# Gate and value products over 32 attention weights, with fp32 halves stacked in the 128 rows

## The chip, the core and the metric

The kernel runs on one core of a Trainium2 chip. The metric is the device time of one execution in microseconds (us), lower is better. TensorE is called PE (its weight loads PEld), VectorE DVE, ScalarE ACT, GpSimd POOL and SyncE SP, whose queue issues the loads and stores.

## What is computed

Two blocks in a row, all in fp32. Attention: x is (4, 12416, 128), the inducing points are (32, 128).

```python
def mab(q, kv):
    s = scale * (q @ kv.transpose(0, 2, 1))
    a = np.exp(s - s.max(-1, keepdims=True))
    a /= a.sum(-1, keepdims=True) + 1e-09
    return a @ kv
h = mab(I, x)          # (4, 32, 128): the inducing points attend to x
x = mab(x, h)          # (4, 12416, 128): x attends to h
```

Then a gated FFN over all 49664 tokens, with weights 128 x 1536, 128 x 1536 and 1536 x 128:

```python
xn = x / np.sqrt(np.mean(x * x, axis=-1, keepdims=True) + 1e-06) * rms_g
g = xn @ w_gate
out = (g / (1 + np.exp(-g)) * (xn @ w_val)) @ w_out
```

A token's x in the FFN is a sum of only 32 rows of h, weighted by its attention weights.

## The kernel before

A batch has 97 blocks of 128 tokens; a unit is four blocks (512 tokens), with one block left over as unit 25. Tokens stand in the columns, the 128 features in the rows. The order of instructions on each engine is the order in which the program writes them; nothing is moved later.

The FFN of a unit (`ffn`, L378) runs 12 slots j, one for each 128 of the 1536 hidden columns. A slot makes the gate product (L403) and the value product (L405), each 128 x 512 with xnT as the moving operand, into two of the four `gv` banks of PSUM. ACT makes silu of the gate (L407), DVE multiplies it by the value (L409) into u. The output product of u (L386) is issued one slot late (`late`), after the next slot's gate and value products, and adds up in `acc` over the 12 slots. Then ACT copies `acc` (L398), and in slot 2 of the next unit PE turns it, DVE copies it (L393) and SP stores it.

Between the products of a slot, `slot` (L430) runs other work: the steps of the next batch's attention, one after another and spread evenly over 24 units, and the seam of the next unit. All of this work shares the two `mm` banks.

The seam makes xnT of a unit: `seam_turn` (slot 1) turns the attention weights of four blocks into [(block, m), token]; `seam_x` (slot 3) multiplies them with a block-diagonal h (`diag`, L348), so that x = a @ h stands with tokens in rows, and POOL squares it; `seam_rms` (slot 5) sums the squares, raises the mean to -0.5 on POOL (L362) and scales x (L364); `seam_end` (slot 8) turns the four blocks (L372) and multiplies by the rms weights (L374).

The attention of a batch: `turn_x` turns x, `scores1` (L191) makes stage 1's scores with four products that use 32 columns of the array each; `max1` to `exp1` (L234) make the exponentials, `turn_e` and `sum_h` (L261) the weighted sums, `end_h` and `turn_h` the result h. `scores2` (L304) makes stage 2's scores as [token, m], one product with 32 columns and its own weight load per block, 16 blocks to a bank; `exp2` (L316) and `norm2` (L329) finish them. The last attention lies under the third batch's FFN.

Batch 0's attention runs ahead of all FFN work and uses the `gv` banks. Between its steps `load_w` (L120) brings in the weights, which come as doubles: SP loads 512 columns, DVE makes eight operations of it and POOL the last (L149).

Of the kernel before, what the change touches and what calls it, by code (L numbers as in the profile page):

```python
# [9 lines left out]
F32 = mybir.dt.float32  # L10
I32 = mybir.dt.int32
U32 = mybir.dt.uint32
AF = mybir.ActivationFunctionType
ALU = mybir.AluOpType
# [4 lines left out]
R = 4  # sets of 32 partitions  # L19
TB = 4  # token blocks of 128 in one 512-wide tile  # L20
GB = R * TB  # token blocks in one attention group


@with_exitstack
def kernel(
# [24 lines left out]
    NG = NB // GB  # L50
    SCALE = float(1.0 / (C ** 0.5))
# [3 lines left out]
    # (first block, number of blocks, sets of blocks, blocks in each)  # L55
# [4 lines left out]
    TAIL0 = NG * TB * P  # first column of the last group's stage 1 scores  # L60
    SCW = TAIL0 + (P if tail else 0)
    units = [(j, min(TB, NB - j)) for j in range(0, NB, TB)]

# [6 lines left out]
    rawp = pool("rawp", 2)  # L70
    small = pool("small", 2)
    work = pool("work", 3)
    seam = pool("seam", 2)
    silp = pool("silp", 4)
# [24 lines left out]
    wg = const.tile([P, F], F32, name="wg")  # L99
    wv = const.tile([P, F], F32, name="wv")  # L100
    wo = const.tile([P, NJ, C], F32, name="wo")
    ident = const.tile([P, P], F32, name="ident")
# [3 lines left out]
    mhalf = const.tile([P, TB], F32, name="mhalf")  # L106
    nc.gpsimd.memset(mhalf[:], -0.5)
    # fold[(q, m), (q', m')] = [m == m']: sums over the sets, into each of them
# [10 lines left out]

    def load_w(i, c):  # L120
# [5 lines left out]
        src, dst = (moe_w_gate, moe_w_val, moe_w_out)[i], (wg, wv, wo.rearrange("p j c -> p (j c)"))[i]  # L126
        dst, k = dst[:, ts(c, 512)], 512 // C
# [4 lines left out]
        raw = rawp.tile([P, 512, 2], I32, name="raw")  # L132
        words = raw[:].rearrange("p f w -> p (f w)")
        nc.sync.dma_start(out=words if i < 2 else words.rearrange("p (j c) -> p j c", j=k), in_=src.bitcast(I32))
        low, high = raw[:, :, 0], raw[:, :, 1]
# [24 lines left out]
    sc, diag = {}, {}  # L160

    def attention(b, load_next):
        """The steps of a batch's attention, in order, up to a in sc[b] and h in diag[b]."""
# [48 lines left out]
        def max2():  # L212
            ps = bank()
            nc.tensor.transpose(ps[0:1, 0:P], st["mx"][:], ident[:])
            row = small.tile([1, m], F32, name="row")
            nc.vector.reduce_max(out=row[:], in_=ps[0:1, 0:P].rearrange("p (q m) -> p m q", m=m), axis=AX.X)
            row4 = small.tile([1, R, m], F32, name="row4")
# [12 lines left out]
        def exp1():  # L230
            s = sc[b]
            hl = st["hl"] = small.tile([P, C + 1], F32, name="hl")
            lt = small.tile([P, 1], F32, name="lt")
            nc.scalar.activation(s[:, 0:TAIL0], s[:, 0:TAIL0], AF.Exp, bias=st["nbias"][:], scale=SCALE,  # L234
                                 accum_out=hl[:, C:C + 1])
            if tail:
                nc.scalar.activation(s[0:m, TAIL0:SCW], s[0:m, TAIL0:SCW], AF.Exp, bias=st["nbias"][0:m],
# [39 lines left out]
        def end_h():  # L277
# [5 lines left out]
            h = st["h"] = small.tile([P, C], F32, name="h")  # L283
            nc.vector.tensor_scalar_mul(out=h[:], in0=ps[:, 0:C], scalar1=rec[:])
            # one block for each of a unit's four blocks of tokens
# [5 lines left out]
        def turn_h():  # L291
            ps = bank()
            nc.tensor.transpose(ps[:, 0:m], st["h"][0:m, :], ident[0:m, 0:m])
            hT = st["hT"] = small.tile([P, m], F32, name="hT")
            nc.vector.tensor_copy(out=hT[:], in_=ps[:, 0:m])

# [3 lines left out]
        def scores2(g):  # L300
            j0, nb, nq, nt = groups[g]
            ps = bank().rearrange("p (j m) -> p j m", m=m)
            for j in range(nb):
                nc.tensor.matmul(ps[:, j, :], xT[:, ts(j0 + j, P)], st["hT"][:], start=True, stop=True)  # L304
            mx = small.tile([P, GB], F32, name="mx2")
            nc.vector.reduce_max(out=mx[:, 0:nb], in_=ps[:, 0:nb, :], axis=AX.X)
            nc.vector.tensor_tensor(
                out=blocks(j0, nb), in0=ps[:, 0:nb, :],
                in1=mx[:, 0:nb].unsqueeze(2).to_broadcast((P, nb, m)), op=ALU.subtract,
            )  # L310

        def blocks(j0, nb):
            return sc[b][:, ds(j0 * m, nb * m)].rearrange("p (j m) -> p j m", m=m)
# [4 lines left out]
        for g in range(len(groups)):  # L318
            add(lambda g=g: scores2(g))
        add(exp2)  # L320

        def norm2(g):
            j0, nb, nq, nt = groups[g]
            a = blocks(j0, nb)
            l2 = small.tile([P, GB], F32, name="l2")
            nc.vector.reduce_sum(out=l2[:, 0:nb], in_=a, axis=AX.X)
            nc.vector.tensor_scalar_add(out=l2[:, 0:nb], in0=l2[:, 0:nb], scalar1=1e-9)
            nc.vector.reciprocal(out=l2[:, 0:nb], in_=l2[:, 0:nb])
            nc.gpsimd.tensor_tensor(out=a, in0=a, in1=l2[:, 0:nb].unsqueeze(2).to_broadcast((P, nb, m)), op=ALU.mult)  # L329

        for g in range(len(groups)):
            add(lambda g=g: norm2(g))
        return steps

    # The seam: xn = x / rms * g of a unit of four blocks, with x = a @ h, transposed.
    st2, xnT = {}, {}

    def seam_turn(b, u):
        j0, nt = units[u]
        ps = ps_m.tile([P, 512], F32, name="mm", tag="mm")  # L340
        nc.tensor.transpose(ps[0:nt * m, 0:P], sc[b][:, ds(j0 * m, nt * m)], ident[:])  # L341
        aT = st2["aT", b, u] = seam.tile([P, P], F32, name="aT")
        nc.vector.tensor_copy(out=aT[0:nt * m, :], in_=ps[0:nt * m, 0:P])  # L343

    def seam_x(b, u):
        j0, nt = units[u]
        ps = ps_m.tile([P, TB, C], F32, name="mm", tag="mm")
        nc.tensor.matmul(ps[:, 0:nt, :], st2.pop(("aT", b, u))[0:nt * m, :], diag[b][0:nt * m, 0:nt, :],  # L348
# [29 lines left out]
    def ffn(b, u, slot):  # L378
# [22 lines left out]
        for j in range(NJ):  # L401
# [8 lines left out]
            if j == 2 and stores:  # L410
                stores.pop()()
# [62 lines left out]
```

## Time and profile before

| what | us |
|---|---|
| median of 3 runs | 3515.55 |
| lowest and highest run | 3512.94, 3516.49 |
| span of the profiled execution | 3520.3 |
| PE busy (98% of the span) | 3443.0 |
| DVE busy (36%) | 1259.5 |
| ACT busy (24%) | 835.7 |
| POOL busy (10%) | 346.6 |

The profile records one execution. Busy times of PE are of pipelined instructions whose ends are modelled, so the distance between starts tells more than a duration. A fp32 product is recorded as two instructions.

### The profile page before, as it was taken

How to read it: one execution, taken by the hardware profiler on the slowest of the kernel's cores; microseconds unless marked ns; L12 is line 12 of the kernel's file. 1: busy time of each engine (PE TensorE's matmuls, PEld its weight loads, DVE VectorE, ACT ScalarE, POOL GpSimd, SP SyncE). 2: the span in 40 equal slices, each digit the busy share in tenths (PEclk: the TensorE clock that was granted, in tenths of full speed). 3: DMA queues.
4: the chain of work that ended last, by engine and by line, in shares of the span. 5: the costliest groups of instructions: out<-in, count | busy, mean ns of one | idle time of the engine just before them, and what ended most of it. 6: DMA issues, size and time to landing. Idle time of an engine off the chain costs nothing.

```text
span 3520.3 us, 28077 instructions
## 1 busy us (share of the span) xinstructions
PE 3443.0 (98%) x10541; PEld 1658.6 (47%) x10541; DVE 1259.5 (36%) x2209; ACT 835.7 (24%) x1398; POOL 346.6 (10%) x364
## 2 busy tenths in 40 slices
PE   5799999999999999999999999999999999999999
PEld 3644444445454444444545444444454444444444
DVE  6333333333333333333343333333334333333333
ACT  1122222221222222222122222222222222222222
POOL 1101000010110001010011101000101100110110
PEclk7699999999999999999999999999999999999999
DMA  4000000110000000010000000000000000000000
GB/s 177 23 9 7 9 6 9 42 46 7 7 10 6 9 6 9 8 55 31 7 9 7 9 7 9 10 6 10 6 7 10 7 9 6 9 9 9 6 9 10
DMA packets 21208, 57.39 MB, mean 16 GB/s; under 512 B 2352, under 2 KB 4944, under 8 KB 18000
## 3 DMA queue, kind: packets, MB, share of 16 engines
q1 hardware_dynamic: 20880, 55.58, 4.4%
q8 instruction: 82, 1.34, 0.2%
q14 instruction: 54, 0.44, 0.0%
q10 hardware_dynamic: 192, 0.02, 0.0%
HBM read 30.16 MB, written 25.43 MB: 16 GB/s over the span
## 4 chain that ended last, share of the span: by engine, by line
PE 96%; DVE 2%; ACT 1%; DMA 1%; issue 0%; POOL 0%; POOLq 0%; ACTq 0%; DVEq 0%
PE acc L386 29%; PE gv L403 28%; PE gv L405 28%; PE mm L348 2%; PE mm L304 2%; PE mm L372 1%; PE mm L391 1%; PE gv L304 1%; PE mm L183 1%; PE mm L261 1%; PE mm L191 1%; DMA raw<-in_moe_w_gate_dram 0%; PE mm L341 0%; PE mm L249 0%; PE gv L261 0%
## 5 line engine op out<-in xcount | busy, mean ns | idle before, releaser
L409 DVE TENSOR_TENSOR u<-silu,gv 128x512 f32<-128x512 f32 (+1 forms) x1200 | 805.3, 672 | 2086.1 <-PE gv L405 1869.0
L407 ACT ACTIVATE silu<-gv 128x512 f32<-128x512 f32 (+1 forms) x1200 | 700.7, 584 | 2399.8 <-PE gv L403 2381.2
L386 PE MATMUL acc<-u,wo 128*128 128x512 f32 (+1 forms) x2400 | 1207.8, 585 | 9.7 <-DVE u L409 9.7
L403 PE MATMUL gv<-xnT,wg 128*128 128x512 f32 (+1 forms) x2400 | 1202.7, 583 | 0.8 <-DVE xnT L374 0.8
L405 PE MATMUL gv<-xnT,wv 128*128 128x512 f32 (+1 forms) x2400 | 1198.4, 581 | 0.0
L403 PEld LDWEIGHTS gv<-xnT,wg 128*128 128x128 f32 x2400 | 454.8, 191 | 556.3 <-issue 554.4
L405 PEld LDWEIGHTS gv<-xnT,wv 128*128 128x128 f32 x2400 | 454.5, 191 | 555.6 <-issue 555.6
L386 PEld LDWEIGHTS acc<-u,wo 128*128 128x128 f32 x2400 | 421.5, 191 | 412.3 <-issue 383.9
L353 POOL TENSOR_TENSOR sq<-xa 128x512 f32<-128x512 f32 (+1 forms) x100 | 101.5, 1015 | 2325.6 <-DVE xa L351 2325.6
L362 POOL TENSOR_TENSOR rs<-ms,mhalf 128x4 f32<-128x4 f32 (+1 forms) x100 | 99.0, 990 | 507.2 <-DVE ms L360 502.1
L348 PE MATMUL mm<-diag,aT 128*128 128x512 f32 (+1 forms) x200 | 101.8, 590 | 6.5 <-DVE aT L343 6.5
L364 POOL TENSOR_TENSOR xa<-xa,rs 128x512 f32<-128x512 f32 (+1 forms) x100 | 101.5, 1015 | 7.9
L398 ACT COPY oT<-acc 128x512 f32<-128x512 f32 (+1 forms) x100 | 57.3, 573 | 111.0 <-PE acc L386 111.0
L374 DVE TENSOR_SCALAR xnT<-mm,gam 128x512 f32<-128x512 f32 (+1 forms) x100 | 72.9, 729 | 7.7 <-PE mm L372 7.5
L372 PEld LDWEIGHTS mm<-ident,xa 128*128 128x128 f32 x388 | 47.9, 142 | 53.8 <-issue 43.2
L351 DVE COPY xa<-mm 128x512 f32<-128x512 f32 (+1 forms) x100 | 67.3, 673 | 16.1 <-PE mm L348 7.8
L304 PEld LDWEIGHTS mm<-hT,xT 128*128 128x128 f32 x582 | 68.5, 193 | 8.6 <-issue 5.7
L391 PEld LDWEIGHTS mm<-ident,oT 128*128 128x128 f32 x388 | 48.5, 141 | 49.8 <-issue 47.7
L372 PE MATMUL mm<-ident,xa 128*128 128x128 f32 x388 | 59.7, 276 | 8.3 <-POOL xa L364 8.3
L393 DVE COPY o<-mm 128x512 f32<-128x512 f32 (+1 forms) x100 | 66.7, 667 | 1.5 <-PE mm L391 1.3
L304 PE MATMUL mm<-hT,xT 128*128 128x32 f32 x582 | 67.2, 274 | 0.0
L359 DVE TENSOR_REDUCE ms<-sq 128x4 f32<-128x512 f32 (+1 forms) x100 | 66.2, 662 | 1.6 <-POOL sq L353 1.2
(123 smaller groups left out, 812.8 us busy)
## 6 DMA issues: line engine op xcount, KB each, us to landing
xn<-in_x_dram SPq DMA_DIRECT2D x24, 1024.0 KB, 5.9
out_dram<-o SPq DMA_DIRECT2D x96, 256.0 KB, 2.0
raw<-in_moe_w_gate_dram SPq DMA_DIRECT2D x3, 512.0 KB, 12.4
raw<-in_moe_w_val_dram SPq DMA_DIRECT2D x3, 512.0 KB, 3.6
raw<-in_moe_w_out_dram SPq DMA_DIRECT2D x3, 512.0 KB, 3.9
xnt<-in_x_dram SPq DMA_DIRECT2D x4, 64.0 KB, 6.3
out_dram<-o SPq DMA_DIRECT2D x4, 64.0 KB, 1.5
ind<-in_inducing_dram ACTq DMA_DIRECT2D x1, 16.0 KB, 3.3
```

Source lines behind the costliest of these rows:

```text
L304: nc.tensor.matmul(ps[:, j, :], xT[:, ts(j0 + j, P)], st["hT"][:], start=True, stop=True)
L348: nc.tensor.matmul(ps[:, 0:nt, :], st2.pop(("aT", b, u))[0:nt * m, :], diag[b][0:nt * m, 0:nt, :], start=True, stop=True)
L353: nc.gpsimd.tensor_tensor(out=sq[:, 0:nt, :], in0=xa[:, 0:nt, :], in1=xa[:, 0:nt, :], op=ALU.mult)
L362: nc.gpsimd.tensor_tensor(out=rs[:, 0:nt], in0=ms[:, 0:nt], in1=mhalf[:, 0:nt], op=ALU.pow)
L364: nc.gpsimd.tensor_tensor(out=xa[:, 0:nt, :], in0=xa[:, 0:nt, :], in1=rs[:, 0:nt].unsqueeze(2).to_broadcast((P, nt, C)), op=ALU.mult)
L372: nc.tensor.transpose(ps[:, ts(t, P)], xa[:, t, :], ident[:])
L386: nc.tensor.matmul(acc[:, 0:T], wo[:, j, :], t[:, 0:T], start=(j == 0), stop=(j == NJ - 1))
L391: nc.tensor.transpose(ps[:, ts(t, P)], oT[:, ts(t, P)], ident[:])
L403: nc.tensor.matmul(g[:, 0:T], wg[:, ts(j, P)], xn[:, 0:T], start=True, stop=True)
L405: nc.tensor.matmul(v[:, 0:T], wv[:, ts(j, P)], xn[:, 0:T], start=True, stop=True)
L407: nc.scalar.activation(s[:, 0:T], g[:, 0:T], AF.Silu)
L409: nc.vector.tensor_tensor(out=t[:, 0:T], in0=s[:, 0:T], in1=v[:, 0:T], op=ALU.mult)
```

## The change

Gate and value products no longer take xn. Since x = a @ h, the gate is (a / rms) @ (h * rms_g) @ w_gate, and the product h * rms_g * w is made once a batch, for 32 rows. The moving operand is then the scaled attention weights, 32 rows of them. Weights and attention weights are each split in a half rounded to the type `F32R` and the rest, also as `F32R`; rows 0 to 63 of the stationary operand hold the first half twice, rows 64 to 127 the second half twice, and the moving operand holds its halves as (first, second, first, second). One product over 128 rows adds up all four half products.

- Units: the last two of a batch have 3 and 2 blocks in place of 4 and 1. Four units make a set.
- `load_w` converts a gate or value slice into a work buffer and SP stores it to DRAM (`w32`); the raw doubles lie in buffers of the scores.
- Stage 2's scores are made like stage 1's, [(q, m), token], copied, and turned (`turn_s`). `norm2` is gone.
- Six steps `stack` a batch read the slices back (`fetch`), multiply them by h and write the two halves. The attention has 75 steps in place of 68, spread over 19 units in place of 24.
- The seam works on a set: x is made only for its squares, which ACT makes; the attention weights are scaled by what also holds the softmax's sum, turned, and split on DVE. Its seven steps lie in the second and third unit of the set before.
- `gather` brings the halves of a unit into 128 rows by four DMAs on SP, in slot 2 of the unit before.
- The output product is issued two slots late in place of one, and the store's turning moves from slot 2 to slot 4.

```diff
+    sizes = [TB] * (NB // TB) + ([NB % TB] if NB % TB else [])
+    if sizes[-1] == 1:
+        sizes[-2:] = [TB - 1, 2]
...
+        dst = work.tile([P, 512], F32, name="w", tag="sq") if i < 2 else wo.rearrange("p j c -> p (j c)")[:, ts(c, 512)]
+        load_w32(i, c, src, dst[:] if i < 2 else dst, k)
+        if i < 2:
+            nc.sync.dma_start(out=w32[i][c][:], in_=dst[:])
...
+            hg = st["hg"] = once.tile([P, P], F32, name="hg")
+            nc.vector.tensor_scalar_mul(out=hg[:], in0=ps[:, 0:P], scalar1=gam[:])
+            stacks[b] = [stk.tile([P, F], F32R, name=n) for n in ("sg", "sv")]
...
+        def scores2(s):
+            ps = bank()
+            for q, u in enumerate(sets[s]):
+                j0, nt = units[u]
+                nc.tensor.matmul(ps[ts(q, m), 0:nt * P], st["hT"][:], xT[:, ds(j0 * P, nt * P)], start=True, stop=True)
+            s2 = st["s2", s] = work.tile([P, 512], F32, name="s2", tag="work")
+            for r0, r1, n in rects(s):
+                evacuate(s2[r0:r1, 0:n], ps[r0:r1, 0:n])
+
+        def turn_s(s):
+            s2, nb = st.pop(("s2", s)), count(s)
+            ps = bank()
+            for t, rows, at in chunks(s):
+                nc.tensor.transpose(ps[:, ds(at, rows)], s2[0:rows, ts(t, P)], ident[0:rows, 0:rows])
...
+        def fetch(i, c):
+            w = st["w", i, c] = work.tile([P, 512], F32, name="w", tag="sq")
+            nc.sync.dma_start(out=w[:], in_=w32[i][c][:])
+
+        def stack(i, c):
+            ps = bank()
+            nc.tensor.matmul(ps[:], st["hg"][:], st.pop(("w", i, c))[:], start=True, stop=True)
+            w = stacks[b][i]
+            nc.vector.tensor_copy(out=w[:, ts(c, 512)], in_=ps[:])
+            nc.vector.tensor_tensor(out=w[H:P, ts(c, 512)], in0=ps[H:P, :], in1=w[H:P, ts(c, 512)].bitcast(F32),
+                                    op=ALU.subtract)
...
+        def turn_a():
+            ps = ps_m.tile([P, 512], F32, name="mm", tag="mm")
+            for t, rows, at in chunks(s):
+                nc.tensor.transpose(ps[0:rows, ts(t, P)], sc[b][:, ds(first(s) * m + at, rows)], ident[:])
+            aT = st["aT"] = once.tile([P, 512], F32, name="aT")
+            for r0, r1, n in rects(s):
+                nc.scalar.copy(out=aT[r0:r1, 0:n], in_=ps[r0:r1, 0:n])
...
+        def square(t, rows, at):
+            k = rows // m
+            ps = ps_m.tile([P, R, C], F32, name="mm", tag="mm")
+            nc.tensor.matmul(ps[:, 0:k, :], st["aT"][0:rows, ts(t, P)], diag[b][0:rows, 0:k, :], start=True, stop=True)
+            sq = work.tile([P, R, C], F32, name="sq", tag="sq")
+            nc.scalar.activation(sq[:, 0:k, :], ps[:, 0:k, :], AF.Square)
+            nc.vector.reduce_sum(out=st["ms"][:, ds(at // m, k)], in_=sq[:, 0:k, :], axis=AX.X)
+
+        def scale():
...
+            nc.gpsimd.tensor_tensor(out=rs[:, 0:nb], in0=ms[:, 0:nb], in1=mhalf[:, 0:nb], op=ALU.pow)
+            a = blocks(b, s)
+            nc.gpsimd.tensor_tensor(out=a, in0=a, in1=rs[:, 0:nb].unsqueeze(2).to_broadcast((P, nb, m)), op=ALU.mult)
+
+        def split():
...
+                nc.vector.tensor_copy(out=hi[r0:r1, 0:n], in_=ps[r0:r1, 0:n])
+                nc.vector.tensor_tensor(out=lo[r0:r1, 0:n], in0=ps[r0:r1, 0:n], in1=hi[r0:r1, 0:n].bitcast(F32),
+                                        op=ALU.subtract)
...
+    def gather(b, u):
+        q, hi, lo = split_of.pop((b, u))
+        T = units[u][1] * P
+        a = moving[b, u] = astk.tile([P, 512], F32R, name="a")
+        for k, half in enumerate((hi, lo, hi, lo)):
+            nc.sync.dma_start(out=a[ts(k, m), 0:T].bitcast(F32), in_=half[ts(q, m), 0:T].bitcast(F32))
...
-            nc.tensor.matmul(g[:, 0:T], wg[:, ts(j, P)], xn[:, 0:T], start=True, stop=True)
+            nc.tensor.matmul(g[:, 0:T], sg[:, ts(j, P)], a[:, 0:T], start=True, stop=True)
             v = ps_gv.tile([P, 512], F32, name="gv", tag="gv")
-            nc.tensor.matmul(v[:, 0:T], wv[:, ts(j, P)], xn[:, 0:T], start=True, stop=True)
+            nc.tensor.matmul(v[:, 0:T], sv[:, ts(j, P)], a[:, 0:T], start=True, stop=True)
...
-            if j == 2 and stores:
+            if j == 4 and stores:
                 stores.pop()()
-            slot(u, j)
-            if late:
-                late.pop()()
+            slot(j)
+            if len(late) > 1:
+                late.pop(0)()
...
+            at = [(1, 1), (1, 4), (1, 7), (1, 10), (2, 1), (2, 4), (2, 10)]
+            for (n, j), f in zip(at, steps):
+                plan.setdefault((b, sets[s][n], j), []).append(f)
...
+        slots, done = sets[-3][-1] * NJ, 0
...
+                if j == 2 and (b, u) in after:
+                    gather(*after[b, u])
```

## Rows read from the trace of the kernel before

**Rows 1.** The page: busy us, share, instructions; the granted clock in 40 slices.
```profile
PE 3443.0 (98%) x10541; PEld 1658.6 (47%) x10541; DVE 1259.5 (36%) x2209; ACT 835.7 (24%) x1398; POOL 346.6 (10%) x364
...
PEclk7699999999999999999999999999999999999999
```

**Rows 2.** The page: the chain that ended last, by engine and by line.
```profile
PE 96%; DVE 2%; ACT 1%; DMA 1%; issue 0%; POOL 0%; POOLq 0%; ACTq 0%; DVEq 0%
PE acc L386 29%; PE gv L403 28%; PE gv L405 28%; PE mm L348 2%; PE mm L304 2%; PE mm L372 1%; PE mm L391 1%; PE gv L304 1%; PE mm L183 1%; PE mm L261 1%; PE mm L191 1%; DMA raw<-in_moe_w_gate_dram 0%; PE mm L341 0%; PE mm L249 0%; PE gv L261 0%
```

**Rows 3.** Timeline of one FFN slot: start, duration, engine, line, operation, [idle before].
```profile
1020.94 1.02 PE L403 MATMUL gv<-xnT,wg 128*128 128x512 f32 x2
...
1021.38 0.19 PEld L405 LDWEIGHTS gv<-xnT,wv 128*128 128x128 f32 x1 [0.24 <-issue]
1021.80 1.02 PE L405 MATMUL gv<-xnT,wv 128*128 128x512 f32 x2
...
1022.00 0.60 ACT L407 ACTIVATE silu<-gv 128x512 f32<-128x512 f32 x1 [1.98 <-PE gv L403]
...
1022.66 1.02 PE L386 MATMUL acc<-u,wo 128*128 128x512 f32 x2
...
1022.93 0.69 DVE L409 TENSOR_TENSOR u<-silu,gv 128x512 f32<-128x512 f32 x1 [1.89 <-PE gv L405]
...
1023.52 0.59 PE L403 MATMUL gv<-xnT,wg 128*128 128x512 f32 x1
```

**Rows 4.** Timeline: the seam's four transpositions between two products.
```profile
1030.82 0.60 PE L372 MATMUL mm<-ident,xa 128*128 128x128 f32 x4
...
1031.26 0.59 PE L386 MATMUL acc<-u,wo 128*128 128x512 f32 x1
```

**Rows 5.** Timeline: column-tiled stage 1 scores, and stage 2 scores of 16 blocks.
```profile
246.18 1.07 PE L191 MATMUL mm<-xT,indT 128*32 128x512 f32 x8
...
247.18 0.70 PE L386 MATMUL acc<-u,wo 128*128 128x512 f32 x1
...
807.43 3.65 PE L304 MATMUL mm<-hT,xT 128*128 128x32 f32 x32
```

**Rows 6.** Groups by line and shape, count | busy us, mean ns | idle before.
```profile
L364 POOL TENSOR_TENSOR xa<-xa,rs 128x512 f32<-128x512 f32 x96 | 99.9, 1041 | 7.6
...
L362 POOL TENSOR_TENSOR rs<-ms,mhalf 128x4 f32<-128x4 f32 x96 | 96.8, 1008 | 490.7 <-DVE ms L360 485.6 <-PE gv L403 5.1
...
L407 ACT ACT_TABLE_LOAD x7 | 9.0, 1283 | 20.8 <-PE gv L403 20.7
...
L362 POOL TENSOR_TENSOR rs<-ms,mhalf 128x1 f32<-128x1 f32 x4 | 2.2, 551 | 16.5 <-DVE ms L360 16.5
```

**Rows 7.** DMA issues by line: count, KB each, median us from issue to landing.
```profile
out_dram<-o SPq DMA_DIRECT2D x96, 256.0 KB, 2.0
...
raw<-in_moe_w_val_dram SPq DMA_DIRECT2D x3, 512.0 KB, 3.6
```

**Rows 8.** Timeline of the start: a slice's conversion, stage 2 scores, the first product.
```profile
20.76 0.43 DVE L140 TENSOR_SCALAR u<-raw 128x512 int32<-128x512 int32 x1 [11.53 <-DMA raw<-in_moe_w_gate_dram]
...
24.93 1.27 POOL L149 TENSOR_TENSOR wg<-silu,u 128x512 f32<-128x512 f32 x1 [23.57 <-DVE silu L148]
...
25.97 0.52 DVE L140 TENSOR_SCALAR u<-raw 128x512 int32<-128x512 int32 x1
...
86.15 41.59 PE L304 MATMUL gv<-hT,xT 128*128 128x32 f32 x194 [0.28 <-DVE hT L295]
...
150.44 2.08 PE L403 MATMUL gv<-xnT,wg 128*128 128x512 f32 x2 [0.84 <-DVE xnT L374]
```

**Rows 9.** Busy us of each engine from 100 to 120, then granted clock, DMA.
```profile
100.00:120.00 20.00, 20.00 (x96) 20.00 (x95) 4.15 (x6) 0.00 (x0) 0.00 (x0) 0.50 0.00 1
```

**Rows 10.** Timeline: the first exponential under the FFN, and PE's wait after it.
```profile
598.77 2.86 ACT L234 ACTIVATE sc<-sc,nbias 128x3072 f32<-128x3072 f32 x1
...
605.25 1.12 PE L386 MATMUL acc<-u,wo 128*128 128x512 f32 x2 [1.88 <-DVE u L409]
```

More of the change, by code (lines that the diff above doesn't have):

```diff
@@ L60, with chunks, rects, first @@
     TAIL0 = NG * TB * P
-    SCW = TAIL0 + (P if tail else 0)
-    units = [(j, min(TB, NB - j)) for j in range(0, NB, TB)]
+    SCW = max(TAIL0 + (P if tail else 0), NB * m)
+    sizes = [TB] * (NB // TB) + ([NB % TB] if NB % TB else [])
+    if sizes[-1] == 1:
+        sizes[-2:] = [TB - 1, 2]
+    units = [(sum(sizes[:u]), n) for u, n in enumerate(sizes)]
+    NU = len(units)
+    sets = [list(range(s, min(s + R, NU))) for s in range(0, NU, R)]
+    def chunks(s):
+        at = 0
+        for t in range(TB):
+            rows = m * sum(units[u][1] > t for u in sets[s])
+            if rows:
+                yield t, rows, at
+            at += rows
+    def rects(s):
+        found = []
+        for q, u in enumerate(sets[s]):
+            n = units[u][1] * P
+            if found and found[-1][2] == n:
+                found[-1][1] = (q + 1) * m
+            else:
+                found.append([q * m, (q + 1) * m, n])
+        return found
+    def first(s):
+        return units[sets[s][0]][0]
+    def count(s):
+        return sum(units[u][1] for u in sets[s])
     def pool(name, bufs, **kw):
@@ L282, in end_h @@
             nc.vector.reciprocal(out=rec[:], in_=rec[:])
[L283 removed]
+            h = st["h"] = once.tile([P, C], F32, name="h")
             nc.vector.tensor_scalar_mul(out=h[:], in0=ps[:, 0:C], scalar1=rec[:])
@@ L331, in attention @@
-        for g in range(len(groups)):
-            add(lambda g=g: norm2(g))
-        return steps
[L336 to L348, printed above, removed]
-                         start=True, stop=True)
-        xa = st2["x", b, u] = seam.tile([P, TB, C], F32, name="xa")
-        nc.vector.tensor_copy(out=xa[:, 0:nt, :], in_=ps[:, 0:nt, :])
-        sq = seam.tile([P, TB, C], F32, name="sq", bufs=1)
-        nc.gpsimd.tensor_tensor(out=sq[:, 0:nt, :], in0=xa[:, 0:nt, :], in1=xa[:, 0:nt, :], op=ALU.mult)
-        st2["sq", b, u] = sq
@@ new lines, in stack @@
+        def stack(i, c):
[5 more added lines that the diff above has]
+                                    op=ALU.subtract)
+        for s in range(len(sets)):
+            add(lambda s=s: scores2(s))
+            if s:
+                add(lambda s=s: turn_s(s - 1))
@@ L422, with slot @@
     assert not weights
[L423 to L425 removed]
+    for f in seam(0, 0):
+        f()
+    gather(0, 0)
+    order = [(b, s) for b in range(B) for s in range(len(sets))]
+    plan = {}
+    for k, (b, s) in enumerate(order):
+        if len(sets[s]) < R:
+            continue
+        following = order[k + 1:k + 3]
+        if following and len(sets[following[0][1]]) < R:
+            steps = seam(*following.pop(0))
+            for i, f in enumerate(steps):
+                plan.setdefault((b, sets[s][0], min(NJ - 1, 2 * i + 1)), []).append(f)
+        if following:
+            steps = seam(*following[0])
+            at = [(1, 1), (1, 4), (1, 7), (1, 10), (2, 1), (2, 4), (2, 10)]
+            for (n, j), f in zip(at, steps):
+                plan.setdefault((b, sets[s][n], j), []).append(f)
+    after = {}
+    flat = [(b, u) for b in range(B) for u in range(NU)]
+    for one, two in zip(flat, flat[1:]):
+        after[one] = two
     for b in range(B):
         steps = attention(b + 1, b + 2 < B) if b + 1 < B else []
[L428 to L440 removed]
+        slots, done = sets[-3][-1] * NJ, 0
+        for u in range(NU):
+            def slot(j):
+                nonlocal done
+                while done < min(len(steps), len(steps) * (u * NJ + j + 1) // slots):
+                    steps[done]()
+                    done += 1
+                for f in plan.get((b, u, j), ()):
+                    f()
+                if j == 2 and (b, u) in after:
+                    gather(*after[b, u])
             ffn(b, u, slot)
[L442 removed]
+    while late:
+        late.pop(0)()
     stores.pop()()
```

140 lines of the change are left out of this document (65 added, 75 removed).

## Prediction

> **What bounds the kernel now.** I read three views first, in this order: the page's busy table and its slices over time, the chain of work that ended last, and the timeline of one step of the FFN loop; then the groups by line and shape and the timeline of the other stages, for prices. The table says PE 98%, DVE 36%, ACT 24%, and the slices show PE full and its granted clock at the top from slice 3 on [rows 1]. The chain is PE for 96%, and 85% of it is three lines in equal parts: gate (L403), value (L405) and output (L386) products [rows 2]. So PE's issue is the bound, and what counts is how long it is held per product. The timeline gives that: one j of the FFN runs from 1020.94 to 1023.52, 2.57 us, in three products of 0.86 us, each of two instructions 0.43 us apart [rows 3]. 0.859 us for 512 columns is 1.68 ns a column, 4.0 cycles at 2.4 GHz. The records overlap by 0.16 us (L405's 1.02 us from 1021.80 ends after L386's start at 1022.66), so I take starts, not durations. The weight load of 0.19 us lies inside a product [rows 3]. ACT and DVE wait for PE: silu and u take 0.60 and 0.69 us per j [rows 3].
>
> **A. Gate and value products.** The work in columns is unchanged: 4 batches of 12416 tokens, 12 j, two products, 1.19 million product columns. What changes is the operand type: halves stacked in 128 rows, so one product gives the sum that full fp32 gives. Before: 1.19 million x 1.68 ns = 1999 us. No row shows a product of the new type. Its slow end is one of today's two instructions, 0.43 us, which saves 999 us. Its quick end is one cycle a column at 2.4 GHz, 0.215 us, which saves 1497 us; four fp32 transpositions of 128 columns, one instruction each, take 0.60 - 0.16 = 0.44 us [rows 4], 2 cycles a column, which speaks for the slow end as the pace at which four bytes stream. For the quick end speaks that the full product takes 4 cycles, and a product of numbers in two halves has 2 x 2 half products: one cycle for each, and the new type needs one. I take the quick end, -1497 us, because it accounts for the 4.0 cycles without a remainder.
> The Trainium skill ("FP8 and Floating Point Precision", section "TensorE Precision Notes") says that true fp32 makes four passes and that a reduced-precision form reads the four bytes and truncates them; by it the saving would be the quick end's.
>
> Weight load: the load of 0.19 us still fits under 0.215 us, but barely; I cost it at nothing. If it doesn't hide, or if PE pauses between the two operand types, what would it cost? The nearest row of a switch in PE's mode is a block of 8 column-tiled instructions (L191) that holds PE from 246.18 to 247.18, 1.00 us, where one full product takes 0.86 [rows 5]: up to 0.14 us for two switches. With two switches per j, 97 units of four blocks x 12 x 0.14 = 163 us. Transposes between products lose nothing beyond their own 0.11 us each [rows 4], and they are nearer, as they use the whole array. So 0, upper end +163; no gain is possible here.
>
> **B. The seam** (a @ h, its rms, the transposition). PE before, per unit of four blocks: one transposition 0.11, one product 0.86, four transpositions 0.44: 1.41 us. After, per set of 16 blocks: 0.44 + 4 x 0.86 + 0.44 = 4.32, or 1.08 per unit. 97 x -0.33 = -32 us. The rest leaves PE's path: squares go to ACT (some 0.6 us each, 97 of them, as silu's record of the same size in [rows 3]), the copies of x and of the scaled x on DVE vanish, POOL's power is done for 16 columns at once. From 1.01 us for 4 columns and 0.55 for one, 16 columns take about 0.55 + 15 x 0.152 = 2.8 us [rows 6]; with the multiplication of 1.04 us [rows 6] it has the six slots between scale and split, 7.7 us, as cover. Without that cover PE would wait 4 us for each of 24 sets, 96 us.
>
> The gather adds four DMAs of 64 KB per unit on SP, issued in slot 2 for the next unit, so 9 slots or 11.6 us ahead; a store of 256 KB lands 2.0 us after its issue [rows 7], and four of them one behind the other take 8. SP's loads and fetches in front of them wait for products that PE has already passed in program order. Cost 0; if a gather came 2 us late each time, 100 x 2 = 200 us, which I hold unlikely.
>
> **C. Stage 2 scores, three batches under the FFN.** 32 short instructions per 16 blocks, each with its own weight load, hold PE 3.65 - 0.16 = 3.49 us [rows 5], 21 us a batch. After: four column-tiled products (as L191, 1.0) and four transpositions (0.44), for 6 sets and a small one 9.2 us. The weights times h add six products of 0.86, 5.2 us. Net -6.8 us a batch, -20 us.
>
> **D. The start, before the first FFN product.** Three things. First, SP now stores each converted gate or value slice before it may issue the next load: it waits for POOL's last step, and queued behind are the next raw weight and, behind that, DVE, which converts in order between the attention's copies. The first conversion starts on DVE at 20.76 and ends on POOL at 26.20; plus 3.6 us for a landing that is 9.0 us a slice, where the next conversion now starts 5.2 us after the first, at 25.97 [rows 7, 8]. Over six slices stage 1's maximum, which is queued on DVE behind eight conversions, comes some 22 us later. Second, the 41.6 us of 194 short instructions at half clock [rows 8, 9] become about 18 us: six times (2 + 0.9) at that clock: -24. Third, the six weight products, at half clock 1.7 us, and the longer chain of the first seam (four square products, the 2.8 us power, the gather) instead of norm and seam: +8. Sum +6, bounds -17 (scores at full clock) and +30.
>
> **E. Exponentials.** Twice a batch ACT loads tables (1.28 us each way) and runs an exponential of 2.86 us [rows 6, 10]; silu stands still 5.4 to 6.2 us. Today PE waits 1.88 us for the first [rows 10]. With four gv banks PE can be two j ahead: that was 5.1 us and becomes 2.6. So each of six stops costs about 4 us, 24 in all, against some 9 now: +15, and up to +30 if the clock falls for a moment after such a gap.
>
> **F. Shorter covers elsewhere.** In a slot of 1.29 us silu ends 1.0 and u 1.75 us after the slot's start; the value product that needs that bank starts at 2.8, the output product (now two j late) at 3.0. Slack about 1 us, more than one 0.69 us DVE instruction. Counted from the code, 75 steps spread over 228 slots, no slot takes three mm banks, and 17 of 300 per batch take two. If each of those 68 cost a DVE instruction, +47; with half a microsecond at each of 100 unit ends, +97. I take +15. The end: two blocks instead of one in the last unit, +2.
>
> **Sum** against the profiled execution: 3520.3 - 1497 - 32 - 20 + 6 + 15 + 15 + 2 = 2009. That execution lies 4.7 us above the median of 3515.55, so about 2005 us.
>
> **Rivals.**
> - *Half rate.* Four-byte operands stream at two cycles a column, as the transpositions do. Then 2005 + 498 = 2503 us. For it: [rows 4]. Against: 4.0 cycles for a full product. 8%.
> - *The clock falls.* In the stretch from 100 to 120 us PE is recorded busy throughout, in instructions of 32 columns, and the granted clock is 0.50, the level of 1.2 GHz [rows 9], so being busy in the record doesn't keep the clock. If the shorter products and the waits of E and F brought it to 1.2 GHz for the whole FFN, the PE work after (1501 us of FFN products, 146 of seam and stores, 130 of attention) doubles to 3554; with 156 before it, 30 of waits and 10 after it, 3750 us: slower. It decides once more than 87% of the FFN phase runs at 1.2 GHz. Against: FFN columns still follow each other without a gap, and slices 3 to 40 all have the full clock [rows 1]. 2.5%. The Trainium skill ("TensorE: Matmul & The Clock Gate", section "A second HAM failure mode: psum-queue depth-cycling") describes small gaps at PSUM banks that make the clock swing; by it some of that loss would come.
> - *The products don't get quicker at all* (the new type is run like fp32): A falls away, 3502 us. 2%.
> - *Square needs its own table on ACT.* Each of 97 squares then stops silu for 1.28 + 0.6 + 1.28 = 3.2 us [rows 3, 6], 0.6 more than the two j in PSUM cover: +58, 2063 us. Against: the 100 copies of oT between silus load none; silu has 7 loads, one at the start and one after each of six exponentials [rows 6]. 3%.
> - *DVE becomes the bound:* excluded. It has 1259.5 us now [rows 1]; new are about 74 us at 0.69 us an instruction (split 33, weights 33, half of the score copies 8), and even with nothing removed, 1334 is below the 1777 us of PE work that the clock rival adds up.
>
> **How the numbers follow.** Forecast 2005 us at 84.5%. Its own range: low, D, E and F at their lower ends (-23, -15, -15) to about 1955; high, +163 for switches or +82 for F with +24 for D and +15 for E, to about 2185. The table rival lies within, the other three outside, 12.5%. Range 1960 to 2185. A measurement can tell 0.2% from no change: faster 0.96 (forecast, tables, half rate and part of the no-gain case), same 0.015, slower 0.025.
>
> **What would show it.** Gate and value instructions half in number and 0.215 us apart (0.43: the half rate; a gap ahead of L386's successor: a switch). Clock at the top in all slices past the start. The first FFN product near 156 us, where it was 150.44 [rows 8]. PE waits behind exponentials of about 4 us, six times. No table load between silu and square. A wait of the first product of a unit for a DMA would prove the gather's cover wrong.

## The result, and the profile after

The changed kernel takes 2007.5 us (median of four runs, 2003.2 to 2009.4) where the kernel before takes 3516.0 (four runs, 3512.9 to 3518.6): a ratio of 0.5706, 95% interval 0.5698 to 0.5715. The prediction was 2005. The sum came out right to 2.5 us, but that is luck in part: three of its terms were off by 7 us or more, and 16 us that the kernel before lost were not in it; the errors cancel, and most of what follows is about that. The page of the profiled execution (span 2004.2 us): busy time by engine, granted clock in 40 slices, chain by engine and by line.

```profile
PE 1910.3 (95%) x7445; PEld 1101.8 (55%) x7445; DVE 1170.0 (58%) x1973; ACT 910.5 (45%) x1550; POOL 116.7 (6%) x92
...
PEclk7589999999999999999999999999999999999999
...
PE 91%; DVE 2%; ACT 2%; issue 1%; DMA 0%; POOL 0%; SPq 0%; ACTq 0%; POOLq 0%; DVEq 0%
PE acc L487 50%; PE gv L506 13%; PE gv L504 13%; PE mm L437 4%; PE mm L492 2%; PE mm L242 2%; PE mm L366 1%; PE mm L320 1%; PE mm L250 1%; PE mm L392 1%; PE mm L454 1%; PE mm L423 1%; ACT L508 0%; PE mm L308 0%; PE mm L375 0%
```

PE is still the bound. What were three equal parts of the chain [rows 2] are now the output product (L487) with 50%, and gate (L504) and value (L506) with 13% each. DVE is at 58% of a span that is much shorter, with about 90 us less work than before [rows 1]. One slot without other work, as in [rows 3] (start, duration, engine, line, operation):

```profile
703.29 0.79 PE L504 MATMUL gv<-a,sg 128*128 128x512 f32 x1
703.69 0.19 PEld L506 LDWEIGHTS gv<-a,sv 128*128 128x128 f32 x1 [0.24 <-issue]
703.92 0.39 PE L506 MATMUL gv<-a,sv 128*128 128x512 f32 x1
704.15 1.02 PE L487 MATMUL acc<-u,wo 128*128 128x512 f32 x2
704.61 0.79 PE L504 MATMUL gv<-a,sg 128*128 128x512 f32 x1
```

Each gate and value product is one instruction (x1) where it was two. From gate to gate it is 1.32 us, where [rows 3] has 2.57. Only value to output (0.23 us) is a clean distance between starts here: a gate product is recorded from 0.03 us behind the start of the output product's second instruction, with its waiting in the 0.79 us. So I take the slot as a whole. Over the slots with no other work its median is 1.318 us at 512 columns (703 slots), 0.994 at 384 and 0.668 at 256; the output product's two instructions are 0.429 us apart, as before.

The groups of the new and the changed steps (line, engine, operation, shapes, count | busy us, mean ns of one | idle time before):

```profile
L504 PE MATMUL gv<-a,sg 128*128 128x512 f32 x1104 | 875.1, 793 | 20.0 <-ACT silu L508 15.3 <-DMA a<-lo 4.7
L506 PE MATMUL gv<-a,sv 128*128 128x512 f32 x1104 | 436.3, 395 | 0.0
...
L447 POOL TENSOR_TENSOR rs<-ms,mhalf 128x16 f32<-128x16 f32 x20 | 58.0, 2902 | 1117.6 <-DVE ms L444 1117.6
L439 ACT ACTIVATE sq<-mm 128x512 f32<-128x512 f32 x92 | 55.0, 598 | 55.9 <-PE mm L437 55.2 <-DVE ms L440 0.6
...
L508 ACT ACT_TABLE_LOAD x7 | 9.0, 1283 | 12.3 <-PE gv L504 12.2
```

Silu still loads its table seven times, as L407 did [rows 6], though 100 of the 104 squares come after the first silu: no square brings a load. The power of 16 columns takes 2.90 us (2.8 forecast from [rows 6]). And the gate and value products wait for a DMA once in the execution, 4.7 us, ahead of the first of all.

### The profile page after: what moved, and what is told of

Same layout as the page of the kernel before. It is cut to its first block, busy times and chain, and to the rows that moved or that the text cites. A ratio compares the mean times of both kernels' runs of the same rounds, so it can differ in the third digit from the quotient of the medians.

```text
span 2004.2 us, 22358 instructions
## 1 busy us (share of the span) xinstructions
PE 1910.3 (95%) x7445; PEld 1101.8 (55%) x7445; DVE 1170.0 (58%) x1973; ACT 910.5 (45%) x1550; POOL 116.7 (6%) x92
## 4 chain that ended last, share of the span: by engine, by line
PE 91%; DVE 2%; ACT 2%; issue 1%; DMA 0%; POOL 0%; SPq 0%; ACTq 0%; POOLq 0%; DVEq 0%
PE acc L487 50%; PE gv L506 13%; PE gv L504 13%; PE mm L437 4%; PE mm L492 2%; PE mm L242 2%; PE mm L366 1%; PE mm L320 1%; PE mm L250 1%; PE mm L392 1%; PE mm L454 1%; PE mm L423 1%; ACT L508 0%; PE mm L308 0%; PE mm L375 0%
## 5 line engine op out<-in xcount | busy, mean ns | idle before, releaser
L510 DVE TENSOR_TENSOR u<-silu,gv 128x512 f32<-128x512 f32 (+2 forms) x1200 | 804.1, 671 | 707.1 <-ACT silu L508 605.5
L487 PE MATMUL acc<-u,wo 128*128 128x512 f32 (+2 forms) x2400 | 1206.1, 584 | 0.0
L508 ACT ACTIVATE silu<-gv 128x512 f32<-128x512 f32 (+2 forms) x1200 | 701.5, 585 | 836.6 <-PE gv L504 454.0
L504 PE MATMUL gv<-a,sg 128*128 128x512 f32 (+2 forms) x1200 | 930.4, 775 | 20.0 <-ACT silu L508 15.3
L487 PEld LDWEIGHTS acc<-u,wo 128*128 128x128 f32 x2400 | 426.0, 189 | 151.6 <-issue 85.9
L506 PE MATMUL gv<-a,sv 128*128 128x512 f32 (+2 forms) x1200 | 466.2, 389 | 0.0
L504 PEld LDWEIGHTS gv<-a,sg 128*128 128x128 f32 x1200 | 228.0, 190 | 298.2 <-issue 216.8
L506 PEld LDWEIGHTS gv<-a,sv 128*128 128x128 f32 x1200 | 228.7, 191 | 274.2 <-issue 197.6
L447 POOL TENSOR_TENSOR rs<-ms,mhalf 128x16 f32<-128x16 f32 (+2 forms) x28 | 71.8, 2564 | 1567.7 <-DVE ms L444 1567.7
L437 PE MATMUL mm<-diag,aT 128*128 128x512 f32 (+1 forms) x208 | 102.1, 574 | 0.8 <-ACT aT L426 0.8
L439 ACT ACTIVATE sq<-mm 128x512 f32<-128x512 f32 (+1 forms) x104 | 59.2, 569 | 57.3 <-PE mm L437 56.3
L494 DVE COPY o<-mm 128x512 f32<-128x512 f32 (+2 forms) x100 | 66.8, 668 | 1.7 <-PE mm L492 1.7
L492 PE MATMUL mm<-ident,oT 128*128 128x128 f32 x388 | 58.6, 272 | 0.5 <-ACT oT L499 0.5
L492 PEld LDWEIGHTS mm<-ident,oT 128*128 128x128 f32 x388 | 48.2, 140 | 13.3 <-ACT oT L499 0.9
L437 PEld LDWEIGHTS mm<-diag,aT 128*128 128x128 f32 (+1 forms) x208 | 36.4, 192 | 11.4 <-issue 4.9
```

Source lines behind the costliest of these rows:

```text
L437: nc.tensor.matmul(ps[:, 0:k, :], st["aT"][0:rows, ts(t, P)], diag[b][0:rows, 0:k, :], start=True, stop=True)
L439: nc.scalar.activation(sq[:, 0:k, :], ps[:, 0:k, :], AF.Square)
L447: nc.gpsimd.tensor_tensor(out=rs[:, 0:nb], in0=ms[:, 0:nb], in1=mhalf[:, 0:nb], op=ALU.pow)
L487: nc.tensor.matmul(acc[:, 0:T], wo[:, j, :], t[:, 0:T], start=(j == 0), stop=(j == NJ - 1))
L492: nc.tensor.transpose(ps[:, ts(t, P)], oT[:, ts(t, P)], ident[:])
L494: nc.vector.tensor_copy(out=o[:, 0:nt, :].rearrange("p t c -> p (t c)"), in_=ps[:, 0:T])
```

## The experiments

Each kernel below is the changed kernel with the edit shown. Those marked (a) ran on one chip beside nine runs of the kernel before (median 3519.1 us), those marked (b) on another beside nine (3516.0); a ratio is taken to those runs, a difference in us to the changed kernel's 2007.5. Distances are between the starts of PE's instructions.

### The operand type alone (a)

```diff
-F32R = mybir.dt.float32r
+F32R = mybir.dt.float32
```

> The changed kernel with its new operand type taken back alone: weights, halves and moving operand are plain fp32, so gate and value products are full fp32 again, over the same 128 rows (the second half is then zero). Theory (the pace of these products is the whole gain): a slot goes from 1.318 us back to 2.575 us; 1164 slots x 1.257 = +1463 us, so 3470 us, some 45 us below the kernel before. Rival (the rearranged seam, scores and lag carry a good part of the gain): below 3300 us. No switch of operand type is left, so gate to value should be 0.429 us apart twice.

Measured: 3441.8 us (3440.9 to 3442.6), ratio 0.9777 [0.9759, 0.9795]. The groups of its gate and value products:

```profile
L504 PE MATMUL gv<-a,sg 128*128 128x512 f32 x2208 | 1129.2, 593 | 4.7 <-DMA a<-lo 4.7
L506 PE MATMUL gv<-a,sv 128*128 128x512 f32 x2208 | 1128.3, 593 | 0.0
```

Twice as many instructions, and a slot of 2.575 us again. Same work, same order, same queues: the operand type is worth 3441.8 - 2007.5 = 1434 us, and all the rest of the change (seam, scores, start, unit sizes) about 77 (3519.1 - 3441.8). It also lets the seam and the scores be compared without the quicker products. I added up, line by line from the first FFN product on, the distance from each PE instruction to the next:

| steps | before | with fp32 operands | difference |
|---|---|---|---|
| seam (L341, L348, L372; now L423, L437, L454) | 141.0 | 103.8 | -37.2 |
| stage 2 scores (L304; now L366, L375, L392) | 63.7 | 43.5 | -20.2 |
| store's turning (L391; now L492) | 48.6 | 42.9 | -5.7 |
| FFN products | 3032.5 | 3016.3 | -16.2 |

Some of this is waits behind exponentials in the kernel before, like that of [rows 10], 8.5 us in all: the three of 1.88 us at stage 1 are the store's turning (5.7), and three of 0.97 us at stage 2 stand in the seam's row, which is -34.3 without them.

The FFN products' 16.2 us I had not listed. Two things in the trace of the kernel before make them up. One is the clock: in eight stretches under the FFN, 27 us together, the granted clock is 0.50, the lower of its two levels, which costs some 14 us. Six of them begin at the end of a block of stage 2's scores in 32-column instructions (128x32 below), two behind an exponential's wait. The tenths of [rows 1] don't show them, since a 9 there means 90% or more. One of the six (timeline; then a stretch with its length, the busy us of PE, PEld, DVE, ACT and POOL, the granted clock, DMA share and GB/s):

```profile
884.72 3.65 PE L304 MATMUL mm<-hT,xT 128*128 128x32 f32 x32
888.21 1.96 PE L386 MATMUL acc<-u,wo 128*128 128x512 f32 x2
...
888.30:891.70 3.40, 3.40 (x6) 1.33 (x6) 1.38 (x2) 0.00 (x0) 0.00 (x0) 0.50 0.00 0
```

The other is the unit of one block: in each of the first three, PE waits 0.29 us for u and 1.08 us for the seam, 4 us together. Clock and waits come to some 18 us; a part of that falls on other lines, such as score instructions that run in the same stretches.

```profile
1004.83 0.66 PE L372 MATMUL mm<-ident,xa 128*128 128x128 f32 x4 [1.08 <-POOL xa L364]
```

The run with fp32 operands has no such unit, no score instructions of 32 columns, no wait for silu or u after 160 us, and not one stretch at the lower clock between 160 and 3430 us. Which of these keeps the clock up was not tried one by one.

### The value product twice (a)

```diff
 nc.tensor.matmul(v[:, 0:T], sv[:, ts(j, P)], a[:, 0:T], start=True, stop=True)
+nc.tensor.matmul(v[:, 0:T], sv[:, ts(j, P)], a[:, 0:T], start=True, stop=True)
```

A slot of 1.318 us less an output product of 0.859 leaves 0.459 for two products, 0.03 more than two times one cycle a column. Either each product takes a little longer, or PE loses it in the change from one operand type to the other. A third product of the new type without a further change of type tells these apart.

> The changed kernel with each value product issued twice (the second writes the same again), which adds one product of the new type right behind one of the same type in each of 1200 slots. It measures that product by itself, and where the 0.030 us go by which a slot is longer than 0.859 + 2 x 0.215 = 1.289 us. If the cost lies in the switches between fp32 and the new type, the added product costs 0.215 us and a slot 1.533 us, total 2007 + 251 = 2258 us. If each product of the new type costs some 0.014 us more than its columns, 0.229 us and 1.547 us, total 2274 us. Half rate would give +500 us.

Measured: 2265.1 us (2264.7 to 2265.4), ratio 0.6434 [0.6426, 0.6443]. The slot:

```profile
910.03 0.80 PE L504 MATMUL gv<-a,sg 128*128 128x512 f32 x1
910.66 0.39 PE L506 MATMUL gv<-a,sv 128*128 128x512 f32 x1
910.89 0.40 PE L507 MATMUL gv<-a,sv 128*128 128x512 f32 x1
911.13 1.02 PE L487 MATMUL acc<-u,wo 128*128 128x512 f32 x2
911.59 0.80 PE L504 MATMUL gv<-a,sg 128*128 128x512 f32 x1
```

The median slot is 1.548 us, 0.230 more; between two products of the same type lie 0.23 us, as between value and output. So it is the product's own pace, and the change of type costs nothing that these rows can tell. The total lies between the two forecasts in part because PE's stops behind exponentials shrink when each slot is longer (10.5 us of waits on silu in place of 14.5), and one of them is followed by a stretch at the lower clock in place of three.

The Trainium skill ("TensorE: Matmul & The Clock Gate", section "Back-to-back issue gap") gives one cycle a column at 2.4 GHz and 2.5 ns for a product by itself, which makes an estimate of 215.8 ns at 512 columns, and a lower figure, 131 ns, for a sustained stream. The measured 229 to 230 ns is 14 ns above the first, so for this type the measurement decides.

### The output product one slot late instead of two (a)

```diff
-            if len(late) > 1:
+            if late:
                 late.pop(0)()
```

> The changed kernel with the output product one slot late, as before, and not two. By the slot's own times u is ready about 1.80 us after its gate product starts and with one slot's lag the output product is due at 1.78 us, so PE waits a little in every slot and up to one DVE instruction of 0.69 us where a step's copy stands ahead of u. Theory (slack of about 1 us is what keeps PE free of waits, and the second slot of lag makes it): +50 to +250 us, with PE waiting for u at the output product's line. Rival (PE has enough other work; the lag makes no difference): within 10 us.

Measured: 2084.4 us (2083.6 to 2085.9), ratio 0.5922 [0.5914, 0.593], 77 us more. Waits of PE from 160 us on (engine, line, waited for: us, times, longest):

```profile
PE acc L487 <- DVE u L510: 30.1, 25, 4.3
```

The named waits are 30 us; much of the rest lies in many short ones: over the 703 slots without other work the median is 1.326 us, hardly more than 1.318, but the mean is 1.422 against 1.335, 61 us. Six of the named waits are the exponentials' stops, 4.3 and 3.1 us where they were 2.7 and 2.15, and the lower clock follows all six, not three. With the longer lag u is nearly always there in time, which is why F of the prediction stayed small.

### The gather without its lead (b)

```diff
-    astk = pool("astk", 3)
+    astk = pool("astk", 1)
...
-            at = [(1, 1), (1, 4), (1, 7), (1, 10), (2, 1), (2, 4), (2, 10)]
+            at = [(1, 1), (1, 4), (1, 7), (1, 10), (2, 1), (2, 4), (3, 1)]
...
-                if j == 2 and (b, u) in after:
+                if j == NJ - 1 and (b, u) in after:
```

> The changed kernel with one buffer for the moving operand in place of three, so that the four gather DMAs of a unit can't start before the last value product of the unit before has read it (gather in slot 11, the split one slot into the next unit). It takes away the cover under which the gather was costed at nothing. Theory: issue of the four takes 2.4 us (0.59 each) and the last lands 2.0 us later; the output product that is left on PE covers 0.9, so PE waits about 3.5 us at each of 99 units: +350 us, +300 to +450, with the first gate product of a unit waiting for a DMA. If such gaps drop the clock for part of a unit, it comes out at the upper end or above. Rival (the transfers are short enough to hide even so): below +100 us.

Measured: 2470.0 us (2469.1 to 2470.8), ratio 0.7023 [0.701, 0.7037], 462 us more. PE's waits from 160 us on:

```profile
PE gv L504 <- DMA a<-lo: 283.6, 95, 3.8
PE gv L504 <- ACT silu L508: 14.3, 6, 2.7
PE gv L504 <- DMA a<-los: 12.9, 4, 3.2
```

The end of one unit in the timeline (PE, and SP's issues of the gather):

```profile
1011.51 1.02 PE L487 MATMUL acc<-u,wo 128*128 128x512 f32 x2
1011.70 0.51 SPq L474 DMA_DIRECT2D a<-hi  x1
...
1013.53 0.59 SPq L474 DMA_DIRECT2D a<-lo  x1
...
1015.79 0.47 PE L504 MATMUL gv<-a,sg 128*128 128x512 f32 x1 [3.26 <-DMA a<-lo]
```

The granted clock by slice on the page:

```profile
PEclk6689998999999999999988999999899999998998
```

And its mean over the span, from the view of the cores:

```profile
core 0: 2469.0 us, clock 0.913
```

The last of the four DMAs is issued 1.83 us after the first, and the product starts 2.26 us after that. Compared slot by slot with the changed kernel, from value product to value product, the step across a unit's end is longer by 3.4 us at the median, 330 us over all unit ends (the waits above are the part of it that the profile names). The two slots behind it are longer by 143 us together, and all the others together shorter by 8. What makes these two slots longer is the lower of the two clock levels: behind 76 of the 99 unit ends the granted clock falls to 0.50 for a while, 89 of 1104 output products have their two instructions more than 0.6 us apart (most of them 0.85, not 0.43), 85 of these in the first 6 us of a unit, where the changed kernel has 5 in all; and the mean clock falls from 0.974 to 0.913. The kernel with its lead shows neither the wait nor the lower clock at any unit end, so the cover that the prediction named is real, and losing it would have cost more than the 200 us put there.

The Trainium skill ("TensorE: Matmul & The Clock Gate", section "HAM oscillation — how this bites in real kernels") describes waits for DMAs between bursts of products after which the clock has dropped each time; this run agrees in kind, at 76 of 99 unit ends.

### Silu in place of the later exponentials (b)

```diff
+            EXP = AF.Silu if b else AF.Exp
...
-            nc.scalar.activation(sc[b][:, 0:NB * m], sc[b][:, 0:NB * m], AF.Exp, scale=SCALE)
+            nc.scalar.activation(sc[b][:, 0:NB * m], sc[b][:, 0:NB * m], AF.Silu if b else AF.Exp, scale=SCALE)
```

`EXP` also stands in stage 1's two exponentials.

> The changed kernel with silu in place of the exponentials of the three attentions that lie under the FFN (another function, not the reference's), so that ACT needs no table loads there while its long instructions stay: silu of the gates stands still about 2.9 to 3.7 us and not 5.4 to 6.2. Compared slot by slot with the run in full fp32 the six stops cost PE 23 us now. Theory E (a stop costs what exceeds two slots): each falls to about 1 us, total -15 to -22 us. Rival (the long instruction alone holds ACT long enough): less than -6 us.

Measured: 1982.6 us (1981.9 to 1984.1), ratio 0.5638 [0.563, 0.5645], 25 us less. The activation of 2.8 us is still there, between two silus; without the two loads PE no longer waits for silu at all. What it takes away, in the changed kernel (ACT's instructions, then PE, then the granted clock behind the stop, in the same form as above):

```profile
494.02 0.60 ACT L508 ACTIVATE silu<-gv 128x512 f32<-128x512 f32 x1
494.64 1.28 ACT L383 ACT_TABLE_LOAD   x1
495.93 2.79 ACT L383 ACTIVATE sc<-sc 128x3104 f32<-128x3104 f32 x1
498.74 1.28 ACT L508 ACT_TABLE_LOAD   x1
500.04 1.09 ACT L508 ACTIVATE silu<-gv 128x512 f32<-128x512 f32 x2
...
500.69 0.50 PE L504 MATMUL gv<-a,sg 128*128 128x512 f32 x1 [2.15 <-ACT silu L508]
...
502.40:505.80 3.40, 3.40 (x8) 1.98 (x7) 1.95 (x4) 0.80 (x2) 0.00 (x0) 0.50 0.71 218
```

Slot by slot the gain is 22 us: 17 are the six stops, and 5 are three stretches like this one, at the lower clock. They begin 0.6 to 1.7 us after the end of a stop (at 502.4, 816.4 and 1454.7), and this run, like the one with fp32 operands, has neither stops nor such stretches.

### The stores of the converted weights on POOL's queue (a)

The start of the changed kernel (DVE's and POOL's instructions, SP's issues):

```profile
20.94 0.43 DVE L199 TENSOR_SCALAR u<-sc 128x512 int32<-128x512 int32 x1 [11.60 <-DMA sc<-in_moe_w_gate_dram]
25.10 1.29 POOL L208 TENSOR_TENSOR w<-silu,u 128x512 f32<-128x512 f32 x1 [23.74 <-DVE silu L207]
26.42 0.33 SPq L181 DMA_DIRECT2D w<-w  x1
26.79 0.43 SPq L192 DMA_DIRECT2D sc<-in_moe_w_gate_dram  x1
30.59 0.43 DVE L199 TENSOR_SCALAR u<-sc 128x512 int32<-128x512 int32 x1 [4.37 <-DMA sc<-in_moe_w_gate_dram]
...
94.74 2.86 ACT L293 ACTIVATE sc<-sc,nbias 128x3072 f32<-128x3072 f32 x1 [24.53 <-DVE nbias L287]
...
126.94 2.79 ACT L383 ACTIVATE sc<-sc 128x3104 f32<-128x3104 f32 x1 [2.98 <-DVE sc L379]
...
149.31 0.76 PE L504 MATMUL gv<-a,sg 128*128 128x512 f32 x1 [4.74 <-DMA a<-lo]
```

SP's store of the converted slice (26.42) waits for POOL's last step, the next raw load (26.79) queues behind it, and DVE waits 4.37 us for that. The edit moves the store off SP:

```diff
-            nc.sync.dma_start(out=w32[i][c][:], in_=dst[:])
+            nc.gpsimd.dma_start(out=w32[i][c][:], in_=dst[:])
```

> The changed kernel with the stores of the converted gate and value slices issued from POOL's queue and not from SP's, so that the next raw weight isn't queued behind POOL's last step. Theory (the start is longer by a serial chain of conversion, store, load, conversion of 9.7 us a slice): the slices come 5.2 us apart again, stage 1's first exponential moves from 94.7 to about 73 us, the first FFN product from 149.3 to about 128 us, and the total falls by 17 to 22 us to about 1988 us. Rival (DVE's conversions or the attention's own chain set the start anyway): less than 4 us.

Measured: 1984.9 us (1982.1 to 1985.6), ratio 0.5635 [0.5627, 0.5643], 22.6 us less. Its start:

```profile
26.00 0.54 DVE L199 TENSOR_SCALAR u<-sc 128x512 int32<-128x512 int32 x1
26.56 0.75 POOL L181 DMA_DIRECT2D w<-w  x1 [0.31 <-POOL w L208]
...
71.68 2.86 ACT L293 ACTIVATE sc<-sc,nbias 128x3072 f32<-128x3072 f32 x1 [18.31 <-DVE nbias L287]
...
126.03 0.77 PE L504 MATMUL gv<-a,sg 128*128 128x512 f32 x1 [4.89 <-DMA a<-lo]
```

The second conversion is back at 26.00, stage 1's exponential comes 23.1 us earlier and the first FFN product 23.3. The whole gain of the run is at the start, as the theory says. With this edit the kernel is quicker than both the kernel before and the changed kernel.

### In addition, the output weights' conversions later (b)

```diff
-            nc.sync.dma_start(out=w32[i][c][:], in_=dst[:])
+            nc.gpsimd.dma_start(out=w32[i][c][:], in_=dst[:])
...
-        if k % 4 == 3 and weights:
+        if k % 4 == 3 and weights and (len(weights) > 3 or k > 36):
```

> The kernel with the stores on POOL's queue, and the three slices of the output weights converted after stage 1's exponential and not ahead of it. Each conversion holds DVE 4.2 us. Theory (at the start DVE's order is the chain): the exponential, at 71.7 us with the stores on POOL's queue, comes 8 to 10 us earlier, of which the copies that now stand behind the conversions in the sums of h give part back; first FFN product from 126.0 to about 120 us, total some 1979 us. Rival (they only move the delay): within 2 us of 1985.

Measured: 1993.7 us (1988.6 to 1994.4), ratio 0.5666 [0.5657, 0.5675]: 9 us more than the version above, which ran on the other chip; the intervals of the ratios don't touch. A miss. Stage 1's exponential does come earlier, at 59.55, but the first FFN product later, at 134.67:

```profile
74.06 0.43 DVE L199 TENSOR_SCALAR u<-sc 128x512 int32<-128x512 int32 x1 [7.32 <-DMA sc<-in_moe_w_out_dram]
78.98 1.94 PE L320 MATMUL gv<-xn,a 128*32 128x128 f32 x32 [8.41 <-DVE a L215]
...
95.04 0.80 PE L338 MATMUL gv<-hl,fold 128*128 128x129 f32 x2 [8.48 <-DVE hl L326]
```

The raw loads now stand on SP behind the next batch's x, and while DVE waits 7.3 us for one, the attention's copies wait behind it in DVE's order, and PE behind those. Moving work off one stretch put it, with its queue, into another.

## Why the prediction was right, term by term

| term | predicted | measured |
|---|---|---|
| A, gate and value products | -1497 | -1463 |
| B, seam | -32 | -34 |
| C, stage 2 scores | -20 | -20 |
| D, start | +6 | -1 |
| E, exponentials | +15 | +14.5 |
| F, shorter covers | +15 | +4 |
| lower clock and waits of before, not listed | 0 | -16 |
| end | +2 | +1 |

The measured terms add up to -1514.5. They are read from the two profiled executions, whose spans differ by 1516.1; the medians differ by 1508.5. The end is counted from the start of the last value product (4.8 us before, 5.8 after).

**A** was right in kind (one cycle a column, one instruction, not the transpositions' pace) and 34 us too large in size. The slot fell by 2.575 - 1.318 = 1.257 us, 1104 times 1388; with 0.941 for each of 48 slots at 384 columns and 0.627 for 48 at 256 it is 1463. The failed step is the quick end itself: 0.215 us a product stands in no row, and it is 0.229, as the value product issued twice showed. Accounting for 4.0 cycles of the full product without a remainder was an argument, not a duration. The half rate (0.43 us) is excluded, and so is the switch of type up to 163 us. The weight load of 0.19 us is hidden.

**B and C** came out to 2 us, from the table of the run with fp32 operands, where no product is recorded early. The first seam is not in it; it belongs to D. The seam's power (2.90 us) has its cover: after 160 us PE waits for nothing but silu, 14.5 us, and once for oT, 0.5. The gather's cover, costed at nothing, is shown by the run without it.

**D** had the mechanism right: the store that waits on SP. Its three parts were off: stage 1's exponential comes 26.7 us later (22 forecast); from there to stage 2's exponential it is 32.2 us where it was 61.1 (68.08 to 129.13), -28.9 (-24 forecast), because from 112 to 125 the granted clock is 0.87, where [rows 9] has 0.50; and from there to the first FFN product 22.4 us instead of 21.3, +1.1 (+8 forecast). I had priced the scores at half clock, and the first seam's longer chain costs next to nothing. The sum of -1 hides 27 us lost, of which the store on POOL's queue gives 23 back.

**E** was right in its sum. Slot by slot against the run with fp32 operands, which has the same order of instructions and no such stop, the six exponentials cost 3.3 us for each of three at stage 1 and 2.7 at stage 2, 18 us. Three of the stops are followed by the lower clock, which the forecast had only in its upper bound; that is 5 us more. So it is 23 us, where before had 8.5, and the 4 us taken for each stop were 3, with the clock 3.8. Silu in place of the exponentials gives 25 us back.

**F** was too large. The same comparison leaves 2 us in the first slots, at the lower clock, and 2 to 3 us over all other slots. Slack of about 1 us was enough; the run with one slot of lag shows what it is without that slack, +77.

**Not listed** was what the kernel before lost under its FFN: some 14 us to the lower clock and 4 us to the waits in its one-block units. The prediction reads [rows 1] as the full clock in all slices from the third on; a 9 there doesn't say that. Six of the eight stretches stand behind the very score instructions that C takes out, so C was worth more than its 20 us. A view of the granted clock around those instructions would have shown it.

**The rivals.** Half rate and no gain are excluded by the slot. The clock rival, the lower level for the whole FFN, is excluded too: from 160 us on the mean granted clock of the changed kernel rounds to 1.00.

```profile
160.00:2004.00 1844.00, 1826.06 (x6949) 1058.32 (x6947) 1087.58 (x1799) 884.31 (x1512) 98.81 (x69) 1.00 0.13 37
```

But its mechanism is there in small: stops of 2.15 and 2.70 us bring the clock down for a moment three times, and the 3 us gaps of the run without lead do it at most unit ends. Square's table is excluded by the count of loads.

The range of 1960 to 2185 was wider than needed. But the 2.5 us between forecast and result are no measure of its steps: A was forecast 34 us too good, and B, D, F and what was not listed together 36 us too bad.

## What to carry to other kernels

Where PE is the bound and its products are in full fp32, a short contraction is an offer: 32 rows leave room in the array for the four products of two halves, and one instruction then does what took four cycles a column. Before taking such a factor into a sum, time the product itself by the distance between starts, once; and when a shorter loop halves every cover, lengthen the lags that feed it by the same factor. A store that waits for a slow engine doesn't belong on the queue that issues the next loads. And read the granted clock in narrow windows around the instructions that a change removes: the tenths of the page hide stretches that were worth some 14 us here.

## What the runs showed of the hardware

- A product of the new type with 512 columns takes 0.229 to 0.230 us, 16 to 17 ns over one cycle a column at 2.4 GHz; a third product adds 0.230 at 512 columns, 0.179 at 384 and 0.117 at 256. Whether the surplus belongs to the product or to its columns these three don't settle. A full fp32 instruction of 512 columns takes 0.429, 2 to 3 ns over two cycles.
- Gaps of about 3 us, one in some 23 us, cost more than their own length: behind 76 of 99 the granted clock fell to 0.50, which added 143 us to 330, and its mean over the span fell from 0.974 to 0.913.
- Shorter stops were enough at times: of six of 2.15 and 2.70 us in the changed kernel three were followed by the lower clock. In the kernel before it fell six times where a block of 32-column products ended, with no gap in PE's record.
- A table load on ACT (1.28 us) stands between two activations without a gap: from the end of silu at 494.62 to the next at 500.04 it is 5.42 us, 1.28 + 2.79 + 1.28 and 0.07 more.
